# A second product in seven quarter products, a group behind the first, with activations in pairs and squares on two engines

## The chip, the cores and the metric

One core of a Trainium2 chip. The metric is the device time of one execution in microseconds (us). Times are medians over the runs of a kernel; a ratio is the mean time of one kernel's fast runs over that of the other's of the same rounds, so it is not quite the ratio of the medians.

## The reference

An attention across channels, then a two-layer feed-forward part on 24,320 tokens of 256 channels:

```python
qn = q / (norm(q, axis=1) + 1e-6);  kn = k / (norm(k, axis=1) + 1e-6)   # per batch, 4 batches
a = softmax(kn.transpose(0, 2, 1) @ qn / tau)                          # 256 x 256 per batch
x = (v @ a).reshape(24320, 256)
h = x @ w_in                                   # 256 -> 2048: the "first product"
g = s * relu(h)**2 + b
out = g @ w_out                                # 2048 -> 256: the "second product"
```

With this draw of the inputs the output is nearly a constant row: `b * w_out.sum(0)` has a standard deviation of 0.0361, all the rest 0.00017 (worked out from the reference). The comparison with the reference therefore says little about the second product.

## The kernel before

The kernel folds the softmax into `w_in` (`wa`, one per batch), so that the first product takes the transposed `v` directly. Gram sums (`q`, `k` products) of the next batch are interleaved. Work goes in steps: 16 per group of 512 tokens, one 128-row tile of h each. The second product follows four steps behind:

```python
LAG = 4
def mm1(s):                                    # one step: 2 matmuls of 512 columns
    h_ps = ps_h.tile([P, TG], FP32, tag="h_ps")            # four PSUM buffers
    ...
    r16 = rpool.tile([P, TG], FP16, tag="r16")
    nc.scalar.activation(out=r16[:, :n], in_=h_ps[:, :n], func=AF.Relu)
def square(s, r16, n):
    nc.vector.tensor_mul(g16[:, :n], r16[:, :n], r16[:, :n])
def mm2(s, h):                                 # 4 matmuls of 256 columns a step (two calls)
    nc.tensor.matmul(o_halves[g, h][:, j % 2, :], g16[:, ts(j, P)], w_out16[:, m, :], ...)
    ...                                        # at m == 15: evacuation by DVE, store
for s in range(NS + LAG + 1):
    made = mm1(s);  mm2(s - LAG, 0);  mm2(s - LAG - 1, 1);  square(s, *made)
    for f in side.pop(s, []): f()              # Gram, norms, weight folding, loads
```

Of the kernel before, what the change touches and what calls it, by code (L numbers as in the profile page):

```python
# [16 lines left out]
def kernel(  # L17
# [31 lines left out]
    LAG = 4  # L49
# [7 lines left out]
    consts = ctx.enter_context(tc.tile_pool(name="consts", bufs=1))  # L57
    wpool = ctx.enter_context(tc.tile_pool(name="wpool", bufs=1))
    qk_pool = ctx.enter_context(tc.tile_pool(name="qk_pool", bufs=6))
    sq_pool = ctx.enter_context(tc.tile_pool(name="sq_pool", bufs=2))  # L60
    f3_pool = ctx.enter_context(tc.tile_pool(name="f3_pool", bufs=7))
    sm_pool = ctx.enter_context(tc.tile_pool(name="sm", bufs=2))
    apool = ctx.enter_context(tc.tile_pool(name="apool", bufs=2))
    vpool = ctx.enter_context(tc.tile_pool(name="vpool", bufs=5))
    vtpool = ctx.enter_context(tc.tile_pool(name="vtpool", bufs=4))
    rpool = ctx.enter_context(tc.tile_pool(name="rpool", bufs=3))
    gpool = ctx.enter_context(tc.tile_pool(name="gpool", bufs=LAG + 4))
    opool = ctx.enter_context(tc.tile_pool(name="opool", bufs=4))

    ps_gram = ctx.enter_context(tc.tile_pool(name="ps_gram", bufs=1, space=bass.MemoryType.PSUM))  # L70
    ps_h = ctx.enter_context(tc.tile_pool(name="ps_h", bufs=4, space=bass.MemoryType.PSUM))
    ps_o = ctx.enter_context(tc.tile_pool(name="ps_o", bufs=3, space=bass.MemoryType.PSUM))
# [4 lines left out]
    w_out32 = wpool.tile([P, FT, C], FP32)  # L77


    JC = 8  # L80
# [11 lines left out]
    chunks_first = make_chunks([JC] * whole + [4, 2, 2])  # L92
    chunks_later = make_chunks([JC] * (whole + 1))

    class Gram:
# [7 lines left out]
        def load(self, c):  # L103
            at, np_, jc = self.chunks[c]
            kc = qk_pool.tile([P, JC, C], FP16, tag="kc", name="kc")
            qc = qk_pool.tile([P, JC, C], FP16, tag="qc", name="qc")
            direct = self.b == 0 and c == 0
            for i, (t, src) in enumerate(((kc, k), (qc, q))):
                rows = src[self.b, at : at + np_ * jc, :].rearrange("(p j) c -> p j c", j=jc)
                if direct:  # L110
                    raw = w_out32[:, ds(i * JC, JC), :]
                    (nc.sync, nc.scalar)[i].dma_start(out=raw, in_=rows)
                else:
                    po(nc.gpsimd.dma_start(out=t[:np_, :jc, :], in_=rows))  # L114
            self.tiles[c] = qc, kc

        def cast(self, c):

            qc, kc = self.tiles[c]
            for h in range(2):  # L120
                js = slice(h * JC // 2, (h + 1) * JC // 2)
                po(nc.vector.tensor_copy(out=kc[:, js, :], in_=w_out32[:, js, :]))  # L122
                po(nc.scalar.copy(out=qc[:, js, :],  # L123
                                  in_=w_out32[:, JC + js.start : JC + js.stop, :]))
# [64 lines left out]
        def add_norms(self, last=False):  # L189

            first = self.n_ps is None
            if first:
                self.n_ps = ps_h.tile([P, 2, CH], FP32, tag="h_ps", name="n_ps")
# [3 lines left out]
            for i, (t, np_, j, a, ch) in enumerate(todo):  # L197
                po(nc.tensor.matmul(self.n_ps[:, a, ch : ch + 1], t[:np_, a, j, ts(ch, P)],  # L198
                                    ones16[:np_, 0:1], start=(first and i == 0),
                                    stop=(last and i == len(todo) - 1), skip_group_check=True))  # L200

        def finish_ops(self):
# [21 lines left out]
            def turn():  # L224
                st["t"] = ps_h.tile([P, CH, C], FP32, tag="h_ps", name="t_ps")
# [13 lines left out]
            def sums():  # L239
                r_ps = ps_h.tile([P, CH], FP32, tag="h_ps", name="r_ps")  # L240
# [10 lines left out]
            def fold_w(f0, n, m):  # L251
                def f():
                    wa_ps = ps_h.tile([P, NW], FP32, tag="h_ps", name="wa_ps")
                    for j in range(CH):
                        po(nc.tensor.matmul(wa_ps[:, :n], st["e"][:, j, ts(m, P)],  # L255
                                            w_in16[:, j, ds(f0, n)],
                                            start=(j == 0), stop=(j == CH - 1)))
                    dst = self.wa[:, m, ds(f0, n)]
                    if m == 0:
                        po(nc.scalar.mul(out=dst, in_=wa_ps[:, :n], mul=st["rs"][:, m : m + 1]))  # L260
                    else:
                        po(nc.vector.tensor_scalar_mul(  # L262
                            out=dst, in0=wa_ps[:, :n], scalar1=st["rs"][:, m : m + 1]))
                return f


            widths = ([NW // 2] * 2 if self.b == 0 else [NW]) + [NW] * (Dff // NW - 1)
            folds, f0 = [], 0
            for n in widths:
                folds += [fold_w(f0, n, m) for m in range(CH)]  # L270
                f0 += n
            return [norms, recip, turn, exps, sums] + folds


# [45 lines left out]
    assert FT == 2 * JC  # L320
    g0.load(0)
    warm = consts.tile([P, 1], FP32)
    po(nc.scalar.activation(out=warm, in_=ones32[:, 0:1], func=AF.Sqrt))
    g0.cast(0)
    for c in range(1, len(g0.chunks)):
        g0.load(c)
# [10 lines left out]
    for h in range(2):  # L337
        po(nc.gpsimd.dma_start(out=w_out32[:, ts(h, FT // 2), :], in_=w_out_rows[:, ts(h, FT // 2), :]))
    load_v(1)
    load_v(2)  # L340
# [4 lines left out]
    s_out = consts.tile([P, 1], FP32)  # L345

# [11 lines left out]
    def keep_busy(n):  # L358

        idle_ps = ps_h.tile([P, TG], FP32, tag="h_ps", name="idle_ps")  # L360
# [11 lines left out]
    for f in fin[3:9]:  # L372
        f()

    def cast_w_out(i):
        part = slice(i * FT // 8, (i + 1) * FT // 8)
        if i % 2:
            po(nc.scalar.copy(out=w_out16[:, part, :], in_=w_out32[:, part, :]))
        else:
            po(nc.vector.tensor_copy(out=w_out16[:, part, :], in_=w_out32[:, part, :]))  # L380

    def rowconst_sum(i, n):
        w = w_out32.rearrange("p f c -> p (f c)")
        a = slice(i * 512, min((i + 1) * 512, n))
        b = slice(n + a.start, n + a.stop)
        po(nc.vector.tensor_add(w[:, a], w[:, a], w[:, b]))

    def rowconst_mm():
        rc_ps = ps_h.tile([P, C], FP32, tag="h_ps", name="rc_ps")
        po(nc.tensor.matmul(rc_ps, ones32, w_out32[:, 0, :], start=True, stop=True))  # L390
        po(nc.vector.tensor_scalar_mul(out=rowconst, in0=rc_ps, scalar1=b_bc))

# [7 lines left out]
    for i, f in enumerate(fin[9:]):  # L400
        at_step(i // 2 * 4 + i % 2 + 1, f)
    at_step(14, lambda: po(nc.vector.tensor_scalar_mul(
        out=s_out, in0=s_bc, scalar1=1.0 / (LAM * LAM))))
    for i in range(8):
        at_step(i + 2, lambda i=i: cast_w_out(i))
    todo = [(i, n) for n in (FT * C // 2, FT * C // 4, FT * C // 8, FT * C // 16)
            for i in range(max(1, n // 512))]
    for i, (part, n) in enumerate(todo):
        at_step(8 + i, lambda part=part, n=n: rowconst_sum(part, n))
    at_step(8 + len(todo), rowconst_mm)  # L410
# [8 lines left out]
    for b in range(1, B):  # L419
        gr = grams[b]  # L420
        w0 = first_group[b - 1] * FT + (18 if b == 1 else 6)
# [26 lines left out]
    NS = NG * FT  # L448
    g16s, o_halves, o_sbs = {}, {}, {}

# [11 lines left out]
    def mm1(s):  # L462
        g, m = divmod(s, FT)
# [3 lines left out]
        h_ps = ps_h.tile([P, TG], FP32, tag="h_ps", name="h_ps")  # L467
# [10 lines left out]
        r16 = rpool.tile([P, TG], FP16, tag="r16", name="r16")  # L478
        po(nc.scalar.activation(out=r16[:, :n], in_=h_ps[:, :n], func=AF.Relu))  # L479
        if m == FT - 1:  # L480
            del vT_tiles[g]
        return r16, n

    def square(s, r16, n):
        g16 = gpool.tile([P, TG], FP16, tag="g16", name="g16")
        po(nc.vector.tensor_mul(g16[:, :n], r16[:, :n], r16[:, :n]))  # L486
        g16s[s] = g16

    def mm2(s, h):

        g, m = divmod(s, FT)
        t0, nj = group(g)
        js = [j for j in (2 * h, 2 * h + 1) if j < nj]
        if not js:
            return
        g16 = g16s[s]
        if m == 0:
            o_halves[g, h] = ps_o.tile([P, 2, C], FP32, tag="o_ps", name="o_ps")
        for j in js:
            po(nc.tensor.matmul(  # L500
                o_halves[g, h][:, j % 2, :], g16[:, ts(j, P)], w_out16[:, m, :],
                start=(m == 0 and j == js[0]), stop=(m == FT - 1 and j == js[-1]),
                skip_group_check=True))
        if m == FT - 1:
            if h == 0:
                o_sbs[g] = opool.tile([P, TG // P, C], FP32, tag="o_sb", name="o_sb")
            o_sb = o_sbs[g]
            po(nc.vector.scalar_tensor_tensor(  # L508
# [8 lines left out]
    for s in range(NS + LAG + 1):  # L517
        made = mm1(s) if s < NS else None

        if 0 <= s - LAG < NS:  # L520
            mm2(s - LAG, 0)
# [42 lines left out]
```

## Time and profile before

| | before |
|---|---|
| time | 759.74 us (759.67 to 759.96, 4 runs) |
| TensorE (PE) busy | 96% of the span of 758.1 us |
| ScalarE (ACT), VectorE (DVE) busy | 69%, 63% |
| a group without Gram work | 13.9 us |
| matmuls, of them second product | 5294, 3040 of 256 columns |

The lines behind it are in the prediction. The way to read them: PE's busy time says little about its pace, because the recorded matmuls overlap (a first-product one is 364 ns long on average, while in a steady stretch they start 216 ns apart); pace is the distance between starts. A group's time is the distance between its first first-product matmul and that of the next group, taken from the trace.

### The profile page before, as it was taken

To read this page: it belongs to the slowest core of one execution; us is meant where nothing else is said; L and a number is where in the kernel's file an instruction comes from. 1 tells how busy PE (TensorE), PEld (TensorE's weight loads), DVE (VectorE), ACT (ScalarE), POOL (GpSimd) and SP (SyncE) were. 2 spreads that over 40 slices of the span, in tenths; PEclk is the share of its full clock that TensorE was granted. 3 is DMA by queue.
4 is the path that set the end of the run, shared out by engine and by line. 5 is a ranking of instruction groups with operands and counts; after the bars stand their busy time and mean duration, and the time that the engine had idled before them with its cause. 6 is when DMAs were issued, how large, how long until landed. Compare 5 with 4: busy or idle time off the path is not lost.

```text
span 758.1 us, 14053 instructions
## 1 busy us (share of the span) xinstructions
PE 730.5 (96%) x5294; PEld 505.3 (67%) x5294; DVE 480.9 (63%) x1063; ACT 520.1 (69%) x861; POOL 57.8 (8%) x112
## 2 busy tenths in 40 slices
PE   2689999999999999999999999999999999999998
PEld 2456666666676666666667666666667766666666
DVE  4777676666556766666566666766565565565565
ACT  4476777776776677776767766677776666666665
POOL 3411100000001000000100001000000000000000
PEclk9999999999999999999999999999999999999999
DMA  9999963337356553326546376233323234312111
GB/s 240 209 229 193 182 152 68 68 84 158 78 116 126 117 137 64 70 63 144 115 99 136 94 119 123 61 86 64 70 60 88 63 70 95 67 52 75 42 63 43
DMA packets 74883, 79.30 MB, mean 105 GB/s; under 512 B 54960, under 2 KB 55792, under 8 KB 74560
## 3 DMA queue, kind: packets, MB, share of 16 engines
q0 software_dynamic: 15200, 39.46, 28.3%
q1 hardware_dynamic: 59472, 37.91, 18.5%
q10 hardware_dynamic: 144, 1.05, 0.4%
q8 instruction: 41, 0.67, 0.4%
q14 instruction: 26, 0.21, 0.1%
HBM read 78.91 MB, written 24.90 MB: 137 GB/s over the span
## 4 chain that ended last, share of the span: by engine, by line
PE 92%; DMA 3%; DVE 2%; ACT 1%; issue 1%; POOL 1%; DVEq 0%; ACTq 0%; POOLq 0%
PE o_ps L500 43%; PE h_ps L476 42%; PE s_ps L133 4%; DMA qc<-in_q_dram 3%; PE wa_ps L255 1%; ACT r L479 1%; DVE f L169 0%; DVE g L486 0%; ACT eT L234 0%; PE n_ps L198 0%; DVE sq L153 0%; POOL kc L114 0%; DVE wa L262 0%; PE t_ps L228 0%; POOL qc L114 0%
## 5 line engine op out<-in xcount | busy, mean ns | idle before, releaser
L479 ACT ACTIVATE r<-h_ps 128x512 f16<-128x512 f32 (+1 forms) x768 | 450.2, 593 | 208.1 <-PE h_ps L476 180.9
L486 DVE TENSOR_TENSOR g<-r 128x512 f16<-128x512 f16 (+1 forms) x768 | 320.6, 420 | 252.2 <-ACT r L479 245.7
L500 PE MATMUL o_ps<-w_out,g 128*128 128x256 f16 x3040 | 457.3, 273 | 0.0
L476 PE MATMUL h_ps<-vT,wa 128*128 128x512 f16 (+7 forms) x1632 | 453.9, 364 | 2.8 <-DVE wa L262 2.0
L500 PEld LDWEIGHTS <-g 128*128 128x128 f16 x3040 | 295.2, 98 | 183.3 <-issue 0.7
L476 PEld LDWEIGHTS <-wa 128*128 128x128 f16 x1632 | 159.3, 98 | 34.8 <-DVE wa L262 3.3
L133 PE MATMUL s_ps<-qc,kc 128*128 128x256 f16 (+1 forms) x384 | 69.4, 283 | 18.9 <-ACT qc L123 10.8
L508 DVE SCALAR_TENSOR_TENSOR o_sb<-o_ps,s_out,rowconst 128x512 f32<-128x512 f32 x95 | 71.1, 748 | 6.4 <-PE o_ps L500 5.6
L284 POOL DMA_DIRECT2D v<-in_v_dram x48 | 25.8, 537 | 576.3 <-DMA vT<-v 484.1
L156 ACT ACTIVATE sq<-kc 128x1024 f16<-128x1024 f16 (+3 forms) x49 | 49.9, 1031 | 10.4 <-DMA kc<-in_k_dram 7.4
L133 PEld LDWEIGHTS <-kc 128*128 128x128 f16 (+1 forms) x384 | 38.9, 101 | 25.4 <-DVE kc L122 10.7
L153 DVE TENSOR_TENSOR sq<-qc 128x1024 f16<-128x1024 f16 (+3 forms) x49 | 32.5, 673 | 1.6 <-DMA qc<-in_q_dram 1.6
L169 DVE TENSOR_TENSOR f<-sq 128x1024 f16<-128x1024 f16 (+1 forms) x47 | 31.9, 685 | 0.7 <-ACT sq L156 0.4
L169 DVE TENSOR_TENSOR f<-f 128x512 f16<-128x512 f16 (+3 forms) x47 | 25.8, 550 | 0.4
L255 PE MATMUL wa_ps<-w_in,eT 128*128 128x512 f16 (+1 forms) x68 | 18.9, 366 | 0.0
L114 POOL DMA_DIRECT2D kc<-in_k_dram x25 | 13.7, 548 | 13.5 <-DMA kc<-in_k_dram 9.6
L114 POOL DMA_DIRECT2D qc<-in_q_dram x25 | 13.7, 547 | 9.3 <-DMA qc<-in_q_dram 3.9
L260 ACT ACTIVATE wa<-wa_ps,rs 128x512 f16<-128x512 f32 (+1 forms) x17 | 11.2, 662 | 4.6 <-PE wa_ps L255 4.6
L262 DVE TENSOR_SCALAR wa<-wa_ps,rs 128x512 f16<-128x512 f32 (+1 forms) x17 | 12.1, 714 | 0.1
L255 PEld LDWEIGHTS <-eT 128*128 128x128 f16 x68 | 6.6, 98 | 1.2
L122 DVE CAST kc<-w_out 128x1024 f16<-128x1024 f32 x2 | 1.3, 689 | 8.8 <-DMA w_out<-in_k_dram 8.8
L123 ACT CAST qc<-w_out 128x1024 f16<-128x1024 f32 x2 | 2.0, 1042 | 7.0 <-DMA w_out<-in_q_dram 7.0
(43 smaller groups left out, 57.0 us busy)
## 6 DMA issues: line engine op xcount, KB each, us to landing
out_dram<-o_sb SPq DMA_DIRECT2D x47, 512.0 KB, 3.0
v<-in_v_dram POOLq DMA_DIRECT2D x47, 256.0 KB, 3.8
kc<-in_k_dram POOLq DMA_DIRECT2D x19, 512.0 KB, 6.7
qc<-in_q_dram POOLq DMA_DIRECT2D x19, 512.0 KB, 8.5
vT<-v SPq DMA_TRANSPOSE x182, 2.4
w_out<-in_moe_w_out_dram POOLq DMA_DIRECT2D x2, 1024.0 KB, 12.2
kc<-in_k_dram POOLq DMA_DIRECT2D x3, 480.0 KB, 5.8
qc<-in_q_dram POOLq DMA_DIRECT2D x3, 480.0 KB, 8.7
```

What stands on the lines that cost most here:

```text
L114: po(nc.gpsimd.dma_start(out=t[:np_, :jc, :], in_=rows))
L133: po(nc.tensor.matmul(self.s_ps[:, ch, :], kc[:np_, j, ts(ch, P)], qc[:np_, j, :], start=(c == 0 and j == 0 and ch == 0), stop=(c == len(s ...
L153: po(nc.vector.tensor_mul(st["sq"][:np_, 0, js, :], qc[:np_, js, :], qc[:np_, js, :]))
L156: po(nc.scalar.activation(out=st["sq"][:np_, 1, js, :], in_=kc[:np_, js, :], func=AF.Square))
L169: po(nc.vector.tensor_add(st["f", half][:np_, arrays], src[:np_, arrays, :half, :], src[:np_, arrays, half : 2 * half, :]))
L255: po(nc.tensor.matmul(wa_ps[:, :n], st["e"][:, j, ts(m, P)], w_in16[:, j, ds(f0, n)], start=(j == 0), stop=(j == CH - 1)))
L284: po(nc.gpsimd.dma_start(out=v16[:, :nj, :], in_=v_flat[t0 : t0 + nj * P, :].rearrange("(p j) c -> p j c", j=nj)))
L476: po(nc.tensor.matmul(dst, wa[:, ci, ts(m, P)], src, start=(ci == 0), stop=(ci == CH - 1), skip_group_check=True))
L479: po(nc.scalar.activation(out=r16[:, :n], in_=h_ps[:, :n], func=AF.Relu))
L486: po(nc.vector.tensor_mul(g16[:, :n], r16[:, :n], r16[:, :n]))
L500: po(nc.tensor.matmul(o_halves[g, h][:, j % 2, :], g16[:, ts(j, P)], w_out16[:, m, :], start=(m == 0 and j == js[0]), stop=(m == FT - 1 an ...
L508: po(nc.vector.scalar_tensor_tensor(out=o_sb[:, js[0] : js[-1] + 1, :], in0=o_halves.pop((g, h)), scalar=s_out, op0=ALU.mult, in1=rowconst ...
```

## The change

The intent is to do less work on the engine that binds. The second product of a group is a 2 x 2 block product (token halves x output halves, with the 2048 rows split into even and odd tiles). Such a product needs seven block products instead of eight, if sums of blocks are formed: T1, T2, T3 and N4 of `w_out` once, and S1 to S4 of the squared activations per group, by DVE. The sums need a whole group, so the second product runs a group behind. Its partial results are gathered in two PSUM banks (X; Z and Y) and evacuated seven times. To relieve DVE, half the squares go to ACT, which in turn takes two tiles per activation. Core of the diff, cut:

```diff
-    LAG = 4
+    NP = FT // 2
+    SHIFT = 3
-    rpool = ...bufs=3, gpool = ...bufs=LAG + 4, vpool 5, vtpool 4, opool 4
-    ps_h = ctx.enter_context(tc.tile_pool(name="ps_h", bufs=4, ...))
+    rpool 2, gpool 2 (a whole group each), spool 1, upool 4, vpool 4, vtpool 3, opool 2
+    ps_h = pool("ps_h", 2, space=PSUM)          # [P, 2, TG]: two banks each
...
+    def sums_of(g, n):                            # [P, 8, 256] each, on DVE
+        if n == 1:   S[1] = A21 + A22
+        elif n == 2: S[2] = S[1] - A11
+        elif n == 3: S[3] = A11 - A21
+        else:        S[4] = A12 - S[2]
...
+        products = [
+            ("X", G(0, 0), W[:, 0, :, lo], p1),       # P1
+            ("Z", lambda: S[1], T1, p5),              # P5
+            ("X", lambda: S[2], T2, p6),              # P6
+            ("Y", G(1, 0), W[:, 1, :, lo], p2),       # P2
+            ("X", lambda: S[3], T3, p7),              # P7
+            ("Z", lambda: S[4], W[:, 1, :, hi], p3),  # P3
+            ("X", G(1, 1), N4, p4),                   # P4
+        ]                          # each: 16 matmuls of 128 columns, then an evacuation
...
+    ON_ACT = (0, 1, 4, 5)                          # pairs squared by ACT
+    plain = {0, NG - 1}                            # first and last group as eight products
+    for s in range(NS + 2 * FT):
+        mm1(g, m)
+        ...                                        # 7 matmuls of group g-1, from m == SHIFT on
+        if m % 2 == 1 and g < NG:
+            relu(g, i)                             # pair i = m // 2, 1024 elements
+        if g < NG and m % 2 == 1 and i - 1 in ON_ACT:
+            square(g, i - 1, i, nc.scalar)
+        if g < NG and m == 8:
+            square(g, 2, 4, nc.vector)
+        if g > 0 and m == 0 and g <= NG:
+            square(g - 1, 6, 8, nc.vector)
+        if 0 < g <= NG and g - 1 not in plain and m in (2, 4, 9, 11):
+            sums_of(g - 1, {2: 1, 4: 2, 9: 3, 11: 4}[m])
+        for f in side.pop(s, []): f()
```

Around it: Gram chunks of 4 rows instead of 8, `w_out` loaded twice (16-bit, and 32-bit in four pieces for the sums), the norm sums in the free half of the X bank, weight folding through one bank.

## The prediction

> **What bounds the kernel now.** I read the page's busy shares first, then the chain of waits, then the groups, then the order of time in a steady stretch.
>
> ```profile
> PE 730.5 (96%) x5294; PEld 505.3 (67%) x5294; DVE 480.9 (63%) x1063; ACT 520.1 (69%) x861; POOL 57.8 (8%) x112
> ...
> PE 92%; DMA 3%; DVE 2%; ACT 1%; issue 1%; POOL 1%; DVEq 0%; ACTq 0%; POOLq 0%
> PE o_ps L500 43%; PE h_ps L476 42%; PE s_ps L133 4%; DMA qc<-in_q_dram 3%; PE wa_ps L255 1%; ACT r L479 1%; DVE f L169 0%; DVE g L486 0%; ACT eT L234 0%; PE n_ps L198 0%; DVE sq L153 0%; POOL kc L114 0%; DVE wa L262 0%; PE t_ps L228 0%; POOL qc L114 0%
> ...
> L479 ACT ACTIVATE r<-h_ps 128x512 f16<-128x512 f32 (+1 forms) x768 | 450.2, 593 | 208.1 <-PE h_ps L476 180.9
> L486 DVE TENSOR_TENSOR g<-r 128x512 f16<-128x512 f16 (+1 forms) x768 | 320.6, 420 | 252.2 <-ACT r L479 245.7
> L500 PE MATMUL o_ps<-w_out,g 128*128 128x256 f16 x3040 | 457.3, 273 | 0.0
> L476 PE MATMUL h_ps<-vT,wa 128*128 128x512 f16 (+7 forms) x1632 | 453.9, 364 | 2.8 <-DVE wa L262 2.0
> ```
>
> PE is the bound: 92% of the chain, and its two products wait 0.0 and 2.8 us in all. ACT and DVE wait for PE (180.9 us) and for each other (245.7 us); their idle time is free. PE's mean of 273 ns is latency, not pace. Pace is read from starts, in time order:
>
> ```profile
> 541.16 0.59 PE L476 MATMUL h_ps<-vT,wa 128*128 128x512 f16 x2
> 541.59 0.60 PE L500 MATMUL o_ps<-w_out,g 128*128 128x256 f16 x4
> 542.03 0.59 PE L476 MATMUL h_ps<-vT,wa 128*128 128x512 f16 x2
> ...
> 545.50 0.74 PE L198 MATMUL n_ps<-ones,f 128*128 128x1 f16 x24
> ```
>
> One step is two first-product matmuls in 0.43 us and four second-product ones in 0.44 us (109 ns each). Sixteen steps, one group of 512 tokens, take 13.9 us. The 24 one-column matmuls, each with its own 128x128 load, take (0.74 - 0.16)/23 = 25 ns a pair, so a load repeats in 25 ns or less. For 128 columns with a load each the sample is the start-up transposes, and for the other engines there are bursts that run unhindered:
>
> ```profile
> 37.33 0.54 PEld L295 LDWEIGHTS <-v 128*128 128x128 f16 x8
> 37.44 0.61 PE L295 MATMUL vT_ps<-ident,v 128*128 128x128 f16 x8
> ```
>
> ```profile
> 11.14 1.28 DVE L153 TENSOR_TENSOR sq<-qc 128x1024 f16<-128x1024 f16 x2
> 11.56 3.89 ACT L156 ACTIVATE sq<-kc 128x1024 f16<-128x1024 f16 x4
> ```
>
> ```profile
> 322.45 0.75 DVE L508 SCALAR_TENSOR_TENSOR o_sb<-o_ps,s_out,rowconst 128x512 f32<-128x512 f32 x1 [0.18 <-PE o_ps L500]
> 323.12 0.41 DVE L486 TENSOR_TENSOR g<-r 128x512 f16<-128x512 f16 x1
> ```
>
> Transposes: (0.61 - 0.219)/7 = 56 ns each, 0.219 being one's recorded length; the load is hidden. Paces: DVE product of 1024 elements 1.28 - 0.68 = 0.60 us; ACT square of 1024 (3.89 - 1.05)/3 = 0.95 us; DVE evacuation of 512 from PSUM 323.12 - 322.45 = 0.67 us.
>
> **What the Trainium skill says.** "TensorE: Matmul & The Clock Gate", Back-to-back issue gap, gives N/2.4 + 2.5 ns for an isolated gap (56 ns at N = 128), but about 81 ns for a sustained stream of load and matmul pairs at N = 128. The eight transposes agree with 56; no long stream of 128-column pairs is in this trace, which is the main risk. "Perfetto Trace Analysis", Optimizing Scalar/DVE Operations, gives a fixed cost of about 60 ns for DVE on SBUF (125 on PSUM) and 93 ns for ScalarE on SBUF (51 on PSUM), half of what durations show. The trace agrees: 0.60 us is 533 ns of elements and 67 more, at two a cycle of 0.96 GHz; 0.95 us is 853 and 94. "VectorE: DVE Perf Modes", What auto-detection actually checks, caps two-input 16-bit operations at two a cycle, which the same 0.60 us shows; the new sums have rows of 256 adjacent elements and should get it.
>
> **The change part by part.** A step stays two first-product matmuls (0.43 us). The second product becomes 7 quarter products x 2 token tiles x 8 = 112 matmuls of 128 columns per group, 7 a step: 7 x 56 = 0.39 us in place of 0.44. A group saves 64 x 109 - 112 x 56 = 6.98 - 6.27 = 0.71 us; the two ends stay plain, so 46 groups save 33 us. All of that lies on PE's path.
>
> Gram work is unchanged in columns: 8 matmuls a group on average, 0.9 us; folding the weights adds 0.3 us and norms 0.1. A mean group should take PE 6.9 + 6.27 + 1.3 = 14.5 us.
>
> ACT: 16 activations of 512 become 8 of 1024. From PSUM I take 853 + 56 = 0.91 us (the before kernel's 512 in 0.48 at pace), so 7.3 us. Four squares of 1024: 3.8. Gram squares, 12 or so per batch over 11.9 groups, 1.0; weights 0.25; tables 0.2. Sum 12.5 us of 14.5.
>
> DVE: two squares of 2048 at 1067 + 65 = 1.13 us: 2.3. Four sums S1 to S4 of 2048: 4.5. Seven evacuations of 256 at 267 + 133 = 0.40: 2.8, in place of two of 0.67. Norms per chunk 0.60 + 0.60 + 0.33 and dependency latencies, 1.8; weights 0.2. Sum 11.6 us of 14.5. Both engines are busier (86% and 80%), neither is the bound on paper.
>
> Waits, counted in steps of 0.82 us (0.90 with Gram). The activation of a pair starts 0.64 us into its second step and takes 1.02; its PSUM buffer is wanted at the start of the third step after, so 2.5 to 2.7 us less 1.66 leave 0.8 to 1.0 us. The squares queued on ACT in two pairs running delay it by 0.1 to 0.4, and a Gram square by 0.95 more: now and then 0.2 us of PE stall, some 4 us in the whole run. The tightest sum is S1: the last DVE square of a group waits for an evacuation at 0.9 us into the next group, ends near 2.5; the last evacuation of the group before ends near 3.1; S1 ends near 4.3, and the second product wants it at 5 x 0.82 + 0.54 = 4.65. It fits, by 0.35 us, and a Gram operation ahead of it mostly falls into the gap before the last evacuation. I allow 3 us. X, Z and Y alternate so that each evacuation has a whole product (1.9 us) to finish.
>
> Start: the chain to the first activation is the same, with fewer PSUM buffers to turn in (+0.7 us). Group 0 has no second product beside it now, and ACT sets its pace: 7.3 + 3.8 + 3 scalings x 0.6 = 12.9 us, with weights taking turns in the two PSUM pairs perhaps 15. Before, about 18 us (39.8 to 57.7) also held 5 us of second product. Net loss 3 us. The three later weight foldings now share one bank, so that each fold waits for the last one's scaling behind activations: 3 x 1.5 = 4 us. The norm matmuls double, +0.6 us a batch: 2 us. The second load of w_out (2 MB) falls where DMA is nearly full; I expect it to land before step 15, but a DVE wait there is possible. The end: PE finishes the plain half group alone, work it had to do anyway, +1 us.
>
> Sum: 759.8 - 33 + 4 + 3 + 0.7 + 3 + 4 + 2 + 1 = 744.5 with every loss paid in full and nothing overlapping. Several of these coincide: a stall on PSUM gives DVE time for S1, and the allowances for stalls and start-up are upper guesses. I take about half of these 17.7 us, 9, and say 736.
>
> **The rivals.** (1) Weight loads don't hide behind 128 columns: 81 ns instead of 56 adds 46 x 112 x 25 ns = 129 us, about 865. Against it: 56 ns in the transposes, 25 ns a pair at one column. (2) ACT becomes the bound: 12.5 us grows past 14.5 if waits on PE leave it idle between bursts, since it must keep order; PSUM pairs are now two in place of four buffers. A stall of 0.5 us in each of 46 groups is 23 us: about 758, unchanged. For it: 86% load and only two buffers; against it: 0.8 us of slack per pair and two light pairs after each heavy two. (3) DVE is late with S1 or an evacuation in every group: 0.3 us x 46 = 14 us more, about 750. (4) Everything hides, only start-up costs are paid: 759.8 - 33 + 3 = 730.
>
> **Range and chances.** 736, with 726 to 753 for rivals 3 and 4 and half of rival 2. Faster by over 2% means under 744.6: 0.77. Rivals 2 and 3 in force give within 2%: 0.17. Only rival 1, or 2 together with 3, is slower by over 2%: 0.06.
>
> **What would show it.** Seven 128-column matmuls per step at 56 ns between starts; a step of 0.82 us without Gram; PE still above 90% of the chain; waits of the first product on the activation, and of the second on S1 and on evacuations, under 10 us together; durations near 1.02 us for the activation, 1.22 for a 2048-element sum, 0.48 for an evacuation. A pace above 60 ns (5 us of time for each ns) or PE waits over 15 us would make the prediction wrong.

## The result, and the profile after

The changed kernel takes 765.44 us (763.81 to 766.93, 4 runs); the ratio to before is 1.0074, interval 1.0050 to 1.0098. The prediction was 736 with a range to 753: wrong, by 29 us.

From the changed kernel's page, busy shares, the chain and two groups:

```profile
PE 719.1 (94%) x7594; PEld 511.2 (67%) x7594; DVE 572.5 (75%) x814; ACT 624.6 (82%) x673; POOL 83.5 (11%) x159
...
PE 53%; ACT 21%; DVE 14%; issue 7%; DMA 4%; SPq 0%; POOL 0%; ACTq 0%; POOLq 0%; DVEq 0%
...
L538 ACT ACTIVATE r<-h_ps 128x1024 f16<-128x1024 f32 (+1 forms) x384 | 387.4, 1014 | 98.9 <-PE h_ps L528 98.3
...
L603 DVE TENSOR_TENSOR S<-g 128x2048 f16<-128x2048 f16 x46 | 55.9, 1215 | 0.0
```

The durations are the predicted ones (1.01 us for an activation, 1.22 for a sum). The chain is not: PE has fallen from 92% of it to 53%, and ACT and DVE have a third, although neither is above 82% busy. So PE waits for engines that are not full. From the changed kernel's view of waits (total us, times, longest):

```profile
PEld L671 <- DVE S L603: 11.9, 23, 0.8
...
PE h_ps L528 <- ACT r L538: 5.3, 10, 1.0
...
PE o_ps L671 <- DVE S L603: 4.5, 21, 0.4
...
PE o_ps L671 <- DVE o_sb L556: 3.5, 7, 0.5
...
PE o_ps L671 <- ACT nrm L221: 2.2, 3, 0.7
```

L603 is S3. L671 is the seven-product matmul (PEld its weight load, so the first and third lines overlap). L556 are the evacuations.

To add it up I went through the matmuls of both traces and took, at each, the distance to the next start less columns/2.4 + 2.5 ns. That form is from the Trainium skill, "TensorE: Matmul & The Clock Gate", Back-to-back issue gap, which gives it for an isolated gap; in this stream too the traces agree with it at 512, 256 and 128 columns (216, 109 and 56 ns). What is left over is time that PE lost by waiting or at half clock:

| PE's time, us | before | after | difference | allowed for in the prediction |
|---|---|---|---|---|
| second product, without waits | 331.8 | 298.0 | -33.8 | -33 |
| norm sums, 112 and 204 loads at 25 ns | 2.8 | 5.1 | +2.3 | +2 |
| start of the first first-product matmul | 39.8 | 42.6 | +2.8 | +0.7 |
| lost in groups 0 and 1 | 4.3 | 12.5 | +8.2 | +3 |
| lost in groups 2 to 46 | 1.5 | 27.1 | +25.6 | +11 |
| lost in group 47, and last matmul to end | 4.1 | 6.4 | +2.3 | +1 |

The differences sum to 7.4 us, with 0.5 of the norm sums counted twice (20 of the added loads fall before the first product); the spans of the two profiled runs differ by 6.5. The saving is there in full. The losses are 39 us where I had listed 15.7 and then counted about half.

In groups 2 to 46 the lost time stood in front of: products with S1, S2 or S3 10.0 us, P3 (with S4) 5.0, first-product matmuls 5.4, P4 2.7, weight folding and its transposes 4.0. Split by product, over all groups: 2.0 us before P5 (S1), 1.0 before P6 (S2), 8.5 before P7 (S3) and 5.2 before P3. A group without Gram took 13.5 us, where 32 x 216 + 112 x 56 ns would be 13.2.

**Where the wait comes from.** One group without Gram, changed kernel, order of time. DVE first (start, length, operation, idle time before it and who ended it):

```profile
602.13 0.48 DVE L556 SCALAR_TENSOR_TENSOR u<-o_ps,s_out,rowconst 128x256 f32<-128x256 f32 x1 [0.67 <-PE o_ps L671]
603.39 1.23 DVE L551 TENSOR_TENSOR g<-r 128x2048 f16<-128x2048 f16 x1 [0.78 <-ACT r L538]
604.54 0.48 DVE L556 SCALAR_TENSOR_TENSOR u<-o_ps,s_out,rowconst 128x256 f32<-128x256 f32 x1
604.93 1.22 DVE L603 TENSOR_TENSOR S<-g 128x2048 f16<-128x2048 f16 x1
```

Then ACT:

```profile
600.49 1.02 ACT L538 ACTIVATE r<-h_ps 128x1024 f16<-128x1024 f32 x1
601.39 1.06 ACT L549 ACTIVATE g<-r 128x1024 f16<-128x1024 f16 x1
602.34 1.02 ACT L538 ACTIVATE r<-h_ps 128x1024 f16<-128x1024 f32 x1
```

Then PE:

```profile
601.28 0.59 PE L528 MATMUL h_ps<-vT,wa 128*128 128x512 f16 x2
...
605.82 0.22 PE L671 MATMUL o_ps<-w_out,g 128*128 128x128 f16 x1
606.20 0.51 PE L671 MATMUL o_ps<-T,S 128*128 128x128 f16 x6 [0.16 <-DVE S L603]
```

Read backwards. P7 could have started 56 ns after 605.82 and started at 606.20: 0.33 us lost. It needs S3, which ran from 604.93. Ahead of S3 in DVE's order is an evacuation, and ahead of that the square of pairs 2 and 3, for which DVE sat idle for 0.78 us until the activation of pair 3 ended (602.34 + 1.02). That activation was late in turn: pair 3's last matmuls start at 601.28, and an unhindered activation starts some 0.63 us after that (604.57 to 605.20 elsewhere in this group), at 601.91. ACT was at the square of pair 1. S3 itself depends on none of this: its inputs are the group before's, squared by 598.1.

That engines take their work in order is what the Trainium skill says ("TensorE: Matmul & The Clock Gate", Architectural detail: ACT and DVE "are strict FIFO"), and this trace agrees: DVE is idle for 0.78 us with S3 ready to run. In Gram groups the norms' additions lengthen the same queue. In group 12, S4, an addition and then two evacuations run without a gap:

```profile
245.34 1.22 DVE L605 TENSOR_TENSOR S<-g,S 128x2048 f16<-128x2048 f16 x1
246.48 0.42 DVE L178 TENSOR_TENSOR f<-f 128x512 f16<-128x512 f16 x1
246.81 0.87 DVE L556 SCALAR_TENSOR_TENSOR o_sb<-o_ps,s_out,u 128x256 f32<-128x256 f32 x2
```

P3 waited there for 0.70 us, until 247.34; it writes the bank that the first of these evacuations reads, and needs S4.

### The profile page after: what moved, and what is told of

The parts are those of the page before. It is cut to its first block, busy times and chain, and to the rows that moved or that the text cites. A ratio compares the mean times of both kernels' runs of the same rounds, so it can differ in the third digit from the quotient of the medians.

```text
span 764.6 us, 17879 instructions
## 1 busy us (share of the span) xinstructions
PE 719.1 (94%) x7594; PEld 511.2 (67%) x7594; DVE 572.5 (75%) x814; ACT 624.6 (82%) x673; POOL 83.5 (11%) x159
## 4 chain that ended last, share of the span: by engine, by line
PE 53%; ACT 21%; DVE 14%; issue 7%; DMA 4%; SPq 0%; POOL 0%; ACTq 0%; POOLq 0%; DVEq 0%
PE h_ps L528 25%; PE o_ps L671 23%; ACT r L538 10%; ACT g L549 8%; PE s_ps L142 4%; DVE S L603 3%; DVE g L551 3%; DVE o_sb L556 2%; DVE u L556 1%; DMA qk<-in_q_dram 1%; ACT sq L165 1%; DVE f L178 1%; DMA raw<-in_k_dram 1%; DMA qk<-in_k_dram 1%; ACT wa L266 1%
## 5 line engine op out<-in xcount | busy, mean ns | idle before, releaser
L538 ACT ACTIVATE r<-h_ps 128x1024 f16<-128x1024 f32 (+1 forms) x384 | 387.4, 1014 | 98.9 <-PE h_ps L528 98.3
L671 PEld LDWEIGHTS <-S 128*128 128x128 f16 x2944 | 197.5, 98 | 101.1 <-DVE S L603 11.9
L671 PEld LDWEIGHTS <-g 128*128 128x128 f16 x2208 | 155.1, 98 | 76.6 <-issue 2.5
L549 ACT ACTIVATE g<-r 128x1024 f16<-128x1024 f16 (+1 forms) x192 | 200.5, 1044 | 0.0
L671 PE MATMUL o_ps<-T,S 128*128 128x128 f16 x2208 | 184.3, 219 | 5.7 <-DVE S L603 4.5
L551 DVE TENSOR_TENSOR g<-r 128x2048 f16<-128x2048 f16 (+1 forms) x96 | 116.2, 1211 | 35.1 <-ACT r L538 34.8
L671 PE MATMUL o_ps<-w_out,g 128*128 128x128 f16 x1472 | 134.7, 219 | 0.0
L556 DVE SCALAR_TENSOR_TENSOR o_sb<-o_ps,s_out,u 128x256 f32<-128x256 f32 x138 | 65.8, 481 | 79.9 <-PE o_ps L671 79.9
L142 PE MATMUL s_ps<-qk 128*128 128x256 f16 (+1 forms) x384 | 74.5, 299 | 15.0 <-ACT qk L133 6.7
L556 DVE SCALAR_TENSOR_TENSOR u<-o_ps,s_out,rowconst 128x256 f32<-128x256 f32 x138 | 66.1, 480 | 28.1 <-PE o_ps L671 27.7
L671 PE MATMUL o_ps<-w_out,S 128*128 128x128 f16 x736 | 63.4, 219 | 3.6 <-DVE o_sb L556 3.5
L671 PE MATMUL o_ps<-N,g 128*128 128x128 f16 x736 | 63.3, 219 | 2.2 <-ACT nrm L221 2.2
L605 DVE TENSOR_TENSOR S<-g,S 128x2048 f16<-128x2048 f16 x46 | 56.0, 1218 | 0.0
L599 DVE TENSOR_TENSOR S<-g 128x2048 f16<-128x2048 f16 x46 | 55.9, 1215 | 0.0
L603 DVE TENSOR_TENSOR S<-g 128x2048 f16<-128x2048 f16 x46 | 55.9, 1215 | 0.0
```

The lines of the kernel that those rows point to most:

```text
L142: po(nc.tensor.matmul(self.s_ps[:, ch, :], kc[:np_, j, ts(ch, P)], qc[:np_, j, :], start=(c == 0 and j == 0 and ch == 0), stop=(c == len(s ...
L538: po(nc.scalar.activation(out=r16[:, :, i % 2, :n], in_=h_tiles.pop((g, i))[:, :, :n], func=AF.Relu))
L549: po(nc.scalar.activation(out=dst, in_=src, func=AF.Square))
L551: po(nc.vector.tensor_mul(dst, src, src))
L556: po(nc.vector.scalar_tensor_tensor(out=dst, in0=src, scalar=s_out, op0=ALU.mult, in1=add, op1=ALU.add))
L599: po(nc.vector.tensor_add(S[1], A21, A22))
```

## The experiments

Theory ("queue"): S3 and S4 come late because they stand behind a square that itself waits for a late activation. Rivals: ACT with its two PSUM pairs is the bound and the waits would only move there; the seven products bring nothing on PE; the loss lies at the ends. Ten kernels passed the comparison, which for the reason given above is weak. The kernel before took 759.76 to 760.46 us (medians) in these rounds.

**s3_early.**

```diff
-    ... and m in (2, 4, 9, 11):  sums_of(g - 1, {2: 1, 4: 2, 9: 3, 11: 4}[m])
+    ... and m in (2, 4, 6, 11):  sums_of(g - 1, {2: 1, 4: 2, 6: 3, 11: 4}[m])
```

> Only S3 moves, from step 9 (behind the DVE square of pairs 2 and 3 and an evacuation) to step 6 (ahead of both). Queue theory: TensorE waits in every group because S3 and S4 stand behind a square that itself waits for a late activation; some 15 us of the changed kernel's 765.4 are such waits. Then the time falls by 10 to 15 us, to 750-755, a group without Gram from 13.5 to 13.2 us. Rival ACT (activations on two PSUM pairs are the bound): waits move to the activation, 763-767. Rival pace (128-column matmuls cost as much as they save): 765.

Measured: 752.64 us, ratio to before 0.9907 (0.9892 to 0.9922). One line moved takes 12.8 us off. The same stretch of a group, s3_early's DVE:

```profile
591.37 1.22 DVE L603 TENSOR_TENSOR S<-g 128x2048 f16<-128x2048 f16 x1
592.50 0.48 DVE L556 SCALAR_TENSOR_TENSOR u<-o_ps,s_out,rowconst 128x256 f32<-128x256 f32 x1
593.39 1.23 DVE L551 TENSOR_TENSOR g<-r 128x2048 f16<-128x2048 f16 x1 [0.41 <-ACT r L538]
594.53 0.48 DVE L556 SCALAR_TENSOR_TENSOR u<-o_ps,s_out,rowconst 128x256 f32<-128x256 f32 x1
594.92 1.22 DVE L605 TENSOR_TENSOR S<-g,S 128x2048 f16<-128x2048 f16 x1
```

and its PE at P7:

```profile
595.81 0.22 PE L671 MATMUL o_ps<-w_out,g 128*128 128x128 f16 x1
595.87 0.50 PE L671 MATMUL o_ps<-T,S 128*128 128x128 f16 x6
```

S3 (L603) fills the idle time ahead of the square, S4 (L605) moves up into S3's place, and P7 follows on time. The activation of pair 3 is as late as before (it starts 1.06 us after its last matmuls do, in both traces), but S3 no longer stands behind it. Lost time before products with sums fell from 15.1 to 2.5 us in groups 2 to 46, and all of what is left stands before P5 and P6 (S1 and S2); a group without Gram takes 13.2 us. The rival "ACT is the bound" predicted no change in time and is out: the loss before first-product matmuls stayed at 5.4 us, it did not grow. The rival "pace" is out as well.

**no_sums.** Its output is wrong, which doesn't matter for the time.

```diff
-    sums_of(g - 1, ...)                          # not called
-    ("Z", lambda: S[1], T1, p5), ("X", lambda: S[2], T2, p6), ("X", lambda: S[3], T3, p7), ("Z", lambda: S[4], ...)
+    ("Z", G(0, 1), T1, p5),      ("X", G(0, 0), T2, p6),      ("X", G(1, 0), T3, p7),      ("Z", G(1, 1), ...)
```

> Wrong result on purpose: the four sums are not computed, the products read unsummed tiles instead; same matmuls, 5 us less DVE work a group. Queue theory: as s3_early or a little below, 747-753, groups without Gram 13.2 us; what is left over 726 is the start, the activation waits and the weight folding. Rival ACT: 761-766. Rival pace: 765.

Measured: 747.43 us (ratio 0.9830). So without any work for the sums the kernel gains 18.0 us, and the place of one sum alone gives 12.8. The other 5.2 are, by the traces, 2.5 in groups 2 to 46, 1.6 before the transposes of the folding, and 1.1 in the last group.

**act_sq_later.** The link to ACT by itself.

```diff
-    if g < NG and m % 2 == 1 and i - 1 in ON_ACT:  square(g, i - 1, i, nc.scalar)
+    # pair 0 after activation 1, pair 1 after activation 3 (was 2), pairs 4, 5 as before
```

> Only the ACT square of pair 1 moves, from ahead of the activation of pair 3 to behind it. Queue theory: activation 3 starts 0.2 us earlier, so the DVE square and S3 behind it come in time: groups without Gram 13.5 to 13.2 us, total 757-762. If the activation's lateness does not gate the DVE queue, the waits for S3 stay at 0.33 us a group: 764-767.

Measured: 755.80 us (ratio 0.9944): 9.6 us less, more than the 3 to 8 that I expected (some 1.6 of it lies in groups 0 and 1, where this run's trace lacks a stretch of half clock that the changed kernel's has; see the start, below). Groups without Gram take 13.2 us although S3 kept its place. The activation now runs without ACT's square ahead of it, and the square comes after. ACT's and DVE's view in the same phase of a group:

```profile
608.39 1.02 ACT L538 ACTIVATE r<-h_ps 128x1024 f16<-128x1024 f32 x1 [0.41 <-PE h_ps L528]
609.31 1.05 ACT L549 ACTIVATE g<-r 128x1024 f16<-128x1024 f16 x1
```

```profile
609.44 1.23 DVE L551 TENSOR_TENSOR g<-r 128x2048 f16<-128x2048 f16 x1 [0.35 <-ACT r L538]
610.59 0.48 DVE L556 SCALAR_TENSOR_TENSOR u<-o_ps,s_out,rowconst 128x256 f32<-128x256 f32 x1
610.98 1.22 DVE L603 TENSOR_TENSOR S<-g 128x2048 f16<-128x2048 f16 x1
```

DVE waits 0.35 us for it instead of 0.78. In groups without Gram either end of the link, ACT's order or DVE's, removes the wait: there the cause is shown from both sides. In the Gram groups 5.1 us before products with sums remain.

**all_plain.** The rest of the change without the seven products.

```diff
-    plain = {0, NG - 1}
+    plain = set(range(NG))
-    self.n_ps = x_tile[0][:, 1, ...]             # no X bank now
+    self.n_ps = ps_o.tile([P, 2, C], FP32, tag="o_ps", name="n_ps")[:, 0, ...]
```

> All groups take the eight-quarter product (64 matmuls of 256 columns); lag of a group, pairs, squares on ACT and DVE stay (norm sums get a PSUM tile of their own, as there is no X bank). TensorE gets 31 us more work and loses the 15 us of waits for sums. Queue theory: 775-785. Rival pace (the seven products bring nothing): 755-765. If the rest of the change cost nothing, it would be 760.

Measured: 772.87 us (ratio 1.0170), 2 us below my range: I had taken away only the waits for sums, but in the trace the waits at P4 and most of those at the folding go too. Two things follow. The restructuring alone costs 13.1 us against before. The seven products were worth 7.4 us in the changed kernel (772.9 to 765.4): of the 33.7 us that they save PE (all matmuls at their pace, waits not counted) some 26 were given back, by the traces 24 of them as lost time in groups 2 to 46. This comparison is not quite clean: all_plain also has the norm sums in a tile of their own, which s3_nps (below) found worth 3.6 us.

**The start: s3_g0, s3_rc_cp, s3_nps.** All on top of s3_early. In the changed kernel PE's order of time shows this after group 0:

```profile
61.13 0.60 PE L577 MATMUL o_ps<-w_out,g 128*128 128x256 f16 x4
64.24 0.70 PE L427 MATMUL rc_ps<-acc,ones 128*128 128x256 f32 x2 [2.51 <-DVE acc L423]
...
66.47 1.06 PE L577 MATMUL o_ps<-w_out,g 128*128 128x256 f16 x4
...
69.49 0.60 PE L577 MATMUL o_ps<-w_out,g 128*128 128x256 f16 x4
```

The row sums for the constant (`rc_ps`) hold PE for 2.5 us, and then the same four matmuls take 1.06 us instead of 0.60 for some 3 us: starts 213 instead of 109 ns apart; the granted clock is 0.50 from 65.7 to 69.1 us. The half clock does not follow from that wait alone: the same wait of 2.51 us stands in the traces of act_sq_later and all_plain, and no half clock comes after it there.

The sums were not late for want of data. The four pieces of `w_out` had landed by 55.7 us, and DVE made the first addition at 56.7. The other additions stood behind a square that waited for an activation, the queue theory once more (DVE's view):

```profile
59.39 1.23 DVE L551 TENSOR_TENSOR g<-r 128x2048 f16<-128x2048 f16 x1 [1.46 <-ACT r L538]
60.53 2.48 DVE L420 TENSOR_TENSOR acc<-acc,w 128x1024 f32<-128x1024 f32 x2
```

The experiments on the start:

```diff
 s3_g0:     square(g, i - 1, i, nc.vector if g == 0 else nc.scalar)
 s3_rc_cp:  at_step(25, rowconst_mm)              # was 20
            nc.vector.tensor_copy(out=T3[...])    # was nc.scalar.copy; T2 too
 s3_nps:    norm sums in a PSUM tile of their own # was the free half of X
```

> s3_early (752.6), with all squares of group 0 on DVE. Start theory: group 0 has no second product beside it and is paced by ACT and the two PSUM pairs; without 4 ACT squares (3.8 us) it falls from 15.0 to about 12 us, total 749-751. If the two PSUM pairs alone pace it, group 0 stays at 15 and the total at 752-754.

Measured: 750.51 us (0.9864), 2.1 less than s3_early. Group 0 fell from 15.0 to 13.5 us, not to 12: ACT paced it in part. In the rest of it the trace shows PE waiting by turns for activations and for DVE's scaling of the weights, which pass through the same two PSUM pairs (0.3 to 0.5 us lost eight times in that group); no run separates these two.

> s3_early (752.6), with the constant-row matmul five steps later (step 25, still before its first reader) and the 8 copies for T2 and T3 on DVE in place of ACT. Start theory: TensorE's 2.7 us wait for the row sums goes, and with it the half clock after it; activations of groups 1 and 2 no longer stand behind copies that wait for DVE. Total 746-749. If this wait only hides another, 751-753.

Measured: 747.22 us (0.9823), 5.4 less. Group 1 fell from 20.8 to 16.5 us and group 2 from 16.4 to 15.0 (its 1.2 us of waits for activations are gone), while group 0 rose from 15.0 to 16.2: the trace has 3.4 us of half clock there (48.9 to 52.4 us), after waits of no more than 1.3 us. The two edits were made together, so what each is worth is not shown. In s3_rc_cp the matmul no longer waits, and there is no half-clock stretch behind it, but the first Gram matmul does wait, because the sums' bank is not yet read:

```profile
65.05 0.60 PE L427 MATMUL rc_ps<-acc,ones 128*128 128x256 f32 x2
...
68.27 0.38 PE L142 MATMUL s_ps<-qk 128*128 128x256 f16 x2 [1.76 <-DVE rowconst L428]
68.49 0.59 PE L528 MATMUL h_ps<-vT,wa 128*128 128x512 f16 x2
```

> s3_early (752.6), with the norm sums in a PSUM tile of their own instead of the spare half of the X bank. The wait of the last product for the square root on ACT (0.9 us in each of three batches) should go: 749.5-751. If the tile turns with X and ZY and delays them, 752-755.

Measured: 749.08 us (0.9848), 3.6 less; I expected 1.6 to 3.1. P4's wait for the square root on ACT is gone (2.7 us to none).

**s3_all and s3_all_rc23.** The three together; then the constant-row matmul at step 23.

> All three on s3_early. If they add: 752.6 - 2.5 - 5 - 2 = 743 (741 to 746), 2% faster than the kernel before. If the start's waits hide one another, 746-749.

Measured: 742.49 us, ratio 0.9766 (0.9749 to 0.9782). The parts add (2.1 + 5.4 + 3.6 = 11.1 expected from the single runs, 10.2 seen). With order and start mended, the kernel is 6 us above the 736 that was predicted.

> s3_all (742.5), with the constant-row matmul at step 23 in place of 25, so that its bank is free when the Gram sums of batch 1 start at step 26. The 1.9 us wait of the first Gram matmul in s3_all should shrink: 740.5-742. If the row sums are late again, 742-744.

Measured: 741.72 us, ratio 0.9766 (0.9752 to 0.9781). The lost time in group 1 fell from 2.6 to 0.8 us, but group 2 lost 1.8 instead of 0.1, before products with sums. The difference of 0.8 us between the medians is within the runs' spread, and the ratios are the same: no gain shown.

**plain_mended.** The eight-quarter product with the same repairs.

> The same mended start and norm sums, but with the eight-quarter product in all groups (all_plain was 772.9). The start's repairs are worth 8 us there too, so 764-766, and the seven products in the mended kernel are worth 22-25 us of the 31 us of TensorE work that they save. If the repairs only helped the seven products, 769-773.

Measured: 764.95 us (ratio 1.0066). The repairs of the start are worth 7.9 us here too, as in the single runs (2.1 + 5.4; the norm sums had their own tile in all_plain already), so they are not about the seven products. Against s3_all_rc23 of the same call the seven products are worth 23.2 us, where they had been worth 7.4 in the comparison above. What is left of the restructuring's cost is 5.2 us.

## Why the prediction was wrong

**What held.** PE was the bound of the kernel before (after the change its share of the chain fell to 53%, where the prediction had looked for over 90%). The pace of 128-column matmuls is 56 ns with a load each; rival 1 (81 ns) did not happen. A step without waits is 0.82 us. The saving of 33 us was measured as 33.8. The durations on ACT and DVE were right. S1 was followed rightly: in the group shown above it ended at 599.81 us and P5 began at 600.17, 0.36 us later, where the prediction had 0.35; its allowance of 3 us is what P5 and P6 lost in the whole run (2.0 + 1.0). One reading was off without consequence: the before kernel's group 0 ended at 57.4 us, not 57.7.

**The step that failed first** is the waits. The prediction says "The tightest sum is S1" and allows 3 us for it. Only S1 was followed through DVE's order; S3 and S4 were not looked at; S3's inputs are ready long before. But their place in the order was behind a square that waits for ACT. The prediction even had the cause in hand: "The squares queued on ACT in two pairs running delay it by 0.1 to 0.4". It asked only whether this delay reaches PE through the PSUM buffer, where there is slack (5.4 us lost, 4 allowed), and not whether it reaches PE through DVE. Products with sums lost 15.1 us in groups 2 to 46 in place of 3; s3_early, which changes the order and nothing else, took 12.6 of these away, and act_sq_later 10. P4's wait for the square root (2.7 us) was not on the list at all; s3_nps removed it.

**The second failed step** is the start. "Net loss 3 us" and "+0.7 us" became 8.2 and 2.8. The wait that the prediction feared, for the load of `w_out`, did not come: the pieces landed by 55.7 us, before the first addition. What PE waited 2.5 us for was the sums of its rows, and they stood in DVE's order behind a square that waited 1.46 us for ACT: the first step's mistake again. s3_rc_cp, with the copies moved to DVE as well, undid 5.4 us.

**The third** is "I take about half of these 17.7 us". The allowances added up to 744.5, and the sum needed more, not less. Nothing in the profile supported that they would overlap: the traces show different groups and different products losing time one after the other.

**Rivals.** Rival 3 named late S1 or evacuations at 0.3 us in 46 groups, about 750. The size per group without Gram came near that, 0.33 us, but by chance, since it was S3 that was late; in Gram groups up to 1.2 us were lost before products with sums. Rival 2 (ACT fills up) was wrong as a bound: with DVE's order mended (s3_early), ACT is 83% busy and the waits do not move to it.

**What stays open.** The first first-product matmul started at 40.6 to 42.9 us in the traces of this family, and 39.8 before. Half-clock stretches during the loads differ from run to run, but no experiment separated them from the smaller chunks. The spread of the changed kernel's runs (3 us, before 0.3) goes with the mean granted clock, 0.985 and 0.989 in the two longer ones and 0.992 and 0.995 in the two shorter ones; four runs do not show that it is the cause. What brings on the half clock after the start is open too: it came with the 2.51 us wait in five of the seven kernels that have this wait. The numerical quality of the seven products was not tested, since the comparison can't see it.

## What to carry to other kernels

When a change makes the binding engine wait for results of engines that keep order, go through every operation that it waits for, not only the one with the latest inputs: what counts is the latest input of anything ahead of it in the same queue. Work that is ready early belongs ahead of work that waits. And allowances for waits that lie in different places add up; don't halve them without a reason in the profile.

## What the Trainium skill lacked or had wrong

- "TensorE: Matmul & The Clock Gate", Back-to-back issue gap, gives about 81 ns a matmul for a sustained stream of load and matmul pairs at 128 columns. Here seven such pairs at a time, 5152 in the run, started 55 to 56 ns apart, (0.55 - 0.219)/6 us; 16 without a break at the end of the run too, (1.06 - 0.219)/15 = 56 ns. The 131 ns that the same sentence gives at 512 columns does not fit either: here it was 216 ns.
- "TensorE: Matmul & The Clock Gate", Why this matters for your kernels, warns of idle gaps over about 3 us. Here shorter ones went with half clock, but not reliably. A wait of 2.51 us had 3.4 us at half pace (213 instead of 109 ns) with it in five kernels, beginning 1.4 us after its end in the changed kernel and half a microsecond before its end in s3_g0. In act_sq_later and all_plain the same wait had none. In s3_rc_cp half clock came after waits of no more than 1.3 us, and none after one of 1.8 us.
- "Perfetto Trace Analysis", Identifying the Most-Contended Engine, judges ACT and DVE by occupancy. With DVE at 75% and ACT at 82% the order of their work cost PE 15 us; moving one sum gave 12.8 us with DVE at 76% and ACT at 83%. I found no page that says how to check an order for an operation that is ready but stands behind one that waits.
